# Two units of a fused attention and feed-forward kernel go up together before they go down, with fewer memsets in the front

## The chip, the cores and the metric

One core of a Trainium2 chip runs the whole program. The metric is device time in microseconds (us). Before the change the median of three runs was 217.9 us (217.55 to 217.96). The profile counts from the first to the last instruction, which is a little shorter: 216.0 us in the profiled run.

Each run also lists the mean clock that was granted to TensorE. A run counts as slow if it is over 1.5% above the fastest run of its kernel; only fast runs are compared. A ratio here is the mean time of one kernel's fast runs over the mean of the other's fast runs in the same rounds on the same chip, so it is not quite the ratio of the medians that are quoted. The interval behind a ratio is its 95% interval.

## The reference, cut to what matters

```python
# attention: B=4, H=8, S=768, D=64; chunks of 32 queries, 16 keys to the left,
# 8 to the right, and 8 memory keys for each head
for c in range(S // 32):
    k_full = concat([mem_k, k[max(0, 32*c - 16) : min(S, 32*c + 40)]])   # v likewise
    out[c] = softmax(q_c @ k_full.T / sqrt(D)) @ v_full
x = out.transpose(0, 2, 1, 3).reshape(B, S, 512)
# feed-forward
xn = (x - mean) / sqrt(var + 1e-6) * g_ln
y = x + relu(xn @ w_ch1) @ w_ch2          # 512 -> 2048 -> 512
```

## The kernel before

The work is cut into 24 tiles of 128 tokens, and three tiles make a unit. A tile passes through **scores** (K times Q on TensorE, exponent on ScalarE), **values** (TensorE), **norm** (VectorE) and **turn_x** (transposes on TensorE, then a copy out of PSUM on ScalarE). A unit then goes **up** (16 products with W1 for each tile, four from each of W1's four quarters) and **down** (4 parts a tile with W2). In the traces of this case TensorE runs these pieces in program order (in the kernel before, a wait of 0.55 us at 29.31 holds all that follows), so the order in which the program lists these pieces is the schedule.

```python
att = [ps.tile([128, 2, 512], FP32, name=f"att{i}") for i in range(2)]  # PSUM: scores, values, transposes
mm = [ps.tile([128, 512], FP32, name=f"mm{i}") for i in range(4)]       # PSUM: up, down

def norm(t, xi):                     # VectorE; p is the att buffer of values(t)
    nc.vector.reciprocal(out=r, in_=free(p, 64, [[128, H]]))
    nc.vector.scalar_tensor_tensor(out=x, in0=p, ..., accum_out=total[i])
    nc.vector.tensor_scalar(out=nmean[i], ...)
    nc.vector.scalar_tensor_tensor(out=xn[i], in0=x, scalar=nmean[i], in1=g_row, ...)

def turn_x(u, i, t, kind="att"):
    pv = ...                         # next att buffer, or a bank of mm
    for dt in range(4):
        nc.tensor.matmul(out=pv[...], lhsT=xn[t % 3][...], rhs=identity, is_transpose=True, ...)
    nc.scalar.copy(out=xT[u % 2][:, :, 128 * i : 128 * i + 128], in_=...)

def up(u, n, hc, t0=0, on_act=False):     # tiles t0 to n-1 of unit u, block hc of 16
    p = slot("mm")[:, 0 : hi - lo]
    for dt in range(4):
        nc.tensor.matmul(out=p, lhsT=..., rhs=xT[u % 2][:, dt, lo:hi], ...)
    # Relu out of PSUM to rT[hc]: odd hc on ScalarE, even hc on VectorE
```

The front (cut to order) clears buffers on VectorE, keeps TensorE busy with filler matmuls (`stay_busy`) while K and Q arrive, attends the first three tiles and takes them up as W1 arrives:

```python
    stay_busy(10)
    clear_v(0, nc.vector, lambda: clear_q(0, 0))
    clear_q(0, 1)
    clear_k(0)
    mem_keys()
    mem_cols(0)
    stay_busy(4)
    # ... loads: W1 quarters 0 to 3, rest of K and Q, W2 with V groups between ...
    turn_x(0, 2, 2)
    for hc in range(4, 8):
        up(0, 2, hc)
    for hc in range(8):
        up(0, 3, hc, 2)
```

Then comes a loop over the units. It takes 16 steps of up and 12 of down, and hangs the attention of the next unit's tiles on the steps of down:

```python
attend(((16, 19, 19, 22), (17, 19, 20, 23), (21, 23, 23, 26)), "att")   # unit 1's plan for unit 2:
                                   # for each tile the steps of scores, values, norm, turn_x
```

The softmax here doesn't subtract the row's maximum and nothing guards it: scores larger than these inputs give would overflow.

Of the kernel before, what the change touches and what calls it, by code (L numbers as in the profile page):

```python
# [15 lines left out]
def kernel(  # L16
# [43 lines left out]
    qraw = [sb.tile([128, 4096], FP16, name=f"qraw{i}") for i in range(2)]  # L60
    QT = kraw[1]
    k16 = [t[0:96, 0:4096].rearrange("p (h r d) -> p h r d", h=H, r=8) for t in kraw]
    q16 = [t[0:96, 0:4096].rearrange("p (h r d) -> p h r d", h=H, r=8) for t in qraw]
# [7 lines left out]
    rT = [sb.tile([128, 384], FP16, name=f"rT{hc}") for hc in range(16)]  # L71
    osb = [sb.tile([128, 512], FP32, name=f"osb{i}") for i in range(3)]
    total = [sb.tile([128, 1], FP32, name=f"total{i}") for i in range(3)]
    nmean = [sb.tile([128, 1], FP32, name=f"nmean{i}") for i in range(3)]
# [29 lines left out]
    def load_kq(b, which, lo=0, hi=96, h0=0, h1=H):  # L104

        dst, src = ((k16, k), (q16, q))[which]
        nc.gpsimd.dma_start(
            out=dst[b % 2][lo:hi, h0:h1, :, :],
            in_=dram(src, (b * H + h0) * HS + 512 * lo,
                     [[512, hi - lo], [HS, h1 - h0], [1, 512]]),  # L110
        )
# [97 lines left out]
    def kq_block(b, j, g0, g1, kind, last=nc.scalar.copy):  # L209
# [7 lines left out]
        for i in range(2):  # L217
            turn_kq(as16(pk[:, i, :]), k16[b % 2], j + i, 96)
        for i in range(2):
            turn_kq(as16(pq[i]), q16[b % 2], j + i, 96)  # L220
# [19 lines left out]
    def load_tokens(b, which, t):  # L240
        dst, src = ((kraw[0], k), (qraw[0], q))[which]
# [11 lines left out]
    def cross_q(half, t0, t1):  # L253
        nc.sync.dma_start_transpose(
            out=free(QT, (24 * half + 4 * t0) * 64, [[64, 4 * (t1 - t0)], [1, 64]]),
            in_=qraw[0][64 * half : 64 * half + 64, 512 * t0 : 512 * t1],
# [59 lines left out]
    def norm(t, xi):  # L316
# [10 lines left out]
            out=nmean[i], in0=total[i], scalar1=-1.0 / 512, scalar2=None, op0=ALU.mult,  # L327
        )
        nc.vector.scalar_tensor_tensor(  # L329
            out=xn[i], in0=x, scalar=nmean[i], in1=g_row, op0=ALU.add, op1=ALU.mult,  # L330
        )

    def root(t, xi):
        i = t % 3
        nc.scalar.activation(  # L335
            out=junk, in_=xs[xi], func=ACTF.Square, bias=nmean[i], accum_out=squares[i],
# [33 lines left out]
    def up(u, n, hc, t0=0, on_act=False):  # L370
# [10 lines left out]
        o = rT[hc][:, lo:hi]  # L381
# [7 lines left out]
    def down(t, i, part):  # L389
# [3 lines left out]
        for hc in range(4 * part, 4 * part + 4):  # L393
            nc.tensor.matmul(  # L394
                out=p, lhsT=rT[hc][:, 128 * i : 128 * i + 128],
# [10 lines left out]
    def down_last(t, i):  # L406

        o = osb[t % 3]
        for lo, hi in ((0, 256), (256, 384), (384, 512)):
            p = slot("mm")[:, 0 : hi - lo]  # L410
            for hc in range(16):
                nc.tensor.matmul(  # L412
                    out=p, lhsT=rT[hc][:, 128 * i : 128 * i + 128],
# [20 lines left out]
    def clear_q(i, par):  # L434

        nc.vector.memset(QZ[i][64 - 64 * par : 128 - 64 * par, :, :, par, :], 0.0)  # L436

    def clear_v(i, eng, between=lambda: None):
# [3 lines left out]
        eng.memset(V[i][:, :, :, 64:HD], 1.0)  # L442
# [20 lines left out]
    nc.vector.memset(memv16[:, :, :, 64:HD], 1.0)  # L463
# [12 lines left out]
    clear_v(0, nc.vector, lambda: clear_q(0, 0))  # L476
    clear_q(0, 1)
    clear_k(0)
    mem_keys()
    mem_cols(0)  # L480
    stay_busy(4)
# [14 lines left out]
    for c in range(4):  # L496
        load_w1(c)
    for which in range(2):
        load_kq(0, which, CUT[which], 96)
    load_w2(0)  # L500
    load_w2(1)
    for g in range(6, 10):
        load_v_group(0, g)
    load_w2(2)
    for g in range(10, NG):
        load_v_group(0, g)
    load_w2(3)
# [11 lines left out]
    for j in range(2):  # L519
        turn_kq(first_k[j], k16[0], j, CUT[0])  # L520
    for j in range(2):
        turn_kq(first_q[j], q16[0], j, CUT[1])
# [5 lines left out]
    for j in range(2, 4):  # L528
        turn_kq(first_k[j], k16[0], j, CUT[0])
# [3 lines left out]
    for j in range(2, 4):  # L533
        turn_kq(first_q[j], q16[0], j, CUT[1])
# [5 lines left out]
    nc.vector.tensor_copy(out=g_row, in_=banks[2])  # L540
    scores(0, 0)
# [21 lines left out]
    turn_x(0, 2, 2)  # L563
    for hc in range(4, 8):
        up(0, 2, hc)
    for hc in range(8):
        up(0, 3, hc, 2)
# [3 lines left out]
    for u, tiles in enumerate(units):  # L571
        n = len(tiles)
        following = units[u + 1] if u + 1 < len(units) else []
        plan = {}

# [3 lines left out]
        def attend(steps, kind="dma"):  # L579

            for i, (s0, s1, s2, s3) in enumerate(steps):
# [5 lines left out]
                at(min(s3 + 3, 27), root, t % 6, t % 9)  # L587
# [11 lines left out]
        if u == 0:  # L599
            at(7, clear_q, 1, 0)  # L600
            at(9, clear_q, 1, 1)
            at(10, clear_k, 1)
            at(23, clear_v, 1, nc.gpsimd)
            for j in (0, 2):
                at(15, kq_block, 0, j, 6, NG, "mm", nc.vector.tensor_copy if j else nc.scalar.copy)
                at(15, keep_rest)
            for t in range(3):
                at(19 + t, root, t, t)
# [96 lines left out]
```

## Time and profile before

| | before |
|---|---|
| median of three runs | 217.9 us |
| span of the profiled run | 216.0 us |
| TensorE (PE) busy | 97% of the span |
| VectorE (DVE), ScalarE (ACT), GpSimd (POOL) busy | 55%, 46%, 48% |
| TensorE's share of the chain that ended last | 94% |

The page's picture in 40 slices of 5.4 us each shows the same in time. Each digit is PE's busy share in tenths, and 9 means 90% or more:

```profile
span 216.0 us, 5059 instructions
...
PE   7999989999999999999999999999999999999993
```

Only the first slice, the sixth (from 27.0 to 32.4 us, with the wait of 0.55 us) and the last show any slack. PE is the bound, and a change can win only what PE waits or spends on fillers.

### The profile page before, as it was taken

The page shows a single profiled execution, that of the slowest core. Times are in us where ns is not written, and L with a number is a line of the kernel's source. Part 1 is how long each engine was busy: PE and PEld are TensorE (multiplying, and loading weights), DVE is VectorE, ACT ScalarE, POOL GpSimd, SP SyncE. Part 2 cuts the span into 40 slices and gives each one's busy share as a digit, 9 for nine tenths or more (in the row PEclk, how much of TensorE's full clock was granted, in tenths as well). Part 3 has the DMA queues.
Part 4 walks back from the last instruction along what each step waited for, and adds up shares of the span by engine and source line. Part 5 has one row for each costly group of instructions (what it writes and reads, how often), then busy time and mean ns, then how long its engine had stood idle before and what let it go on. Part 6 is the DMA issues. An engine that isn't in the chain of part 4 may idle for free.

```text
span 216.0 us, 5059 instructions
## 1 busy us (share of the span) xinstructions
PE 210.2 (97%) x2011; PEld 129.8 (60%) x2011; DVE 118.6 (55%) x274; ACT 99.7 (46%) x206; POOL 104.4 (48%) x185
## 2 busy tenths in 40 slices
PE   7999989999999999999999999999999999999993
PEld 2557866557765577546754676456754675466562
DVE  6967675685737548524375349224484447634222
ACT  4478437855893677302653167103761275314100
POOL 7993245699996318974004998507145000400000
PEclk9999999999999999999999999999999999999998
DMA  5999999999999989996312999997674101330012
GB/s 78 182 150 207 209 208 181 200 206 226 148 140 172 102 135 146 151 146 171 48 27 80 142 186 148 138 156 103 176 150 132 49 3 24 91 108 0 0 49 100
DMA packets 87714, 27.37 MB, mean 127 GB/s; under 512 B 78297, under 2 KB 84185, under 8 KB 87642
## 3 DMA queue, kind: packets, MB, share of 16 engines
q0 software_dynamic: 62128, 14.38, 78.2%
q1 hardware_dynamic: 25562, 12.66, 28.2%
q8 instruction: 16, 0.26, 0.5%
q14 instruction: 8, 0.07, 0.1%
HBM read 28.84 MB, written 6.29 MB: 163 GB/s over the span
## 4 chain that ended last, share of the span: by engine, by line
PE 94%; DVE 3%; ACT 1%; issue 1%; ACTq 0%
PE mm L377 37%; PE mm L394 37%; PE att L289 5%; PE att L309 3%; PE mm L366 3%; PE att L179 2%; PE mm L412 2%; PE mm L179 1%; DVE QZ L436 1%; ACT AT L296 1%; PE att L352 1%; PE att L366 1%; DVE rT L385 1%; PE mm L539 0%; DVE xn L329 0%
## 5 line engine op out<-in xcount | busy, mean ns | idle before, releaser
L377 PE MATMUL mm<-xT,w1c 128*128 128x384 f16 (+2 forms) x560 | 89.0, 313 | 0.6 <-DVE rT L385 0.6
L394 PE MATMUL mm<-w2c,rT 128*128 128x512 f16 x368 | 84.4, 379 | 0.0
L377 PEld LDWEIGHTS <-w1c 128*128 128x128 f16 x560 | 58.8, 114 | 23.6 <-issue 1.0
L383 ACT ACTIVATE rT<-mm 128x384 f16<-128x384 f32 (+2 forms) x74 | 33.1, 453 | 72.4 <-PE mm L377 50.2
L394 PEld LDWEIGHTS <-rT 128*128 128x128 f16 x368 | 34.7, 98 | 37.5
L385 DVE TENSOR_SCALAR rT<-mm 128x384 f16<-128x384 f32 (+2 forms) x66 | 34.9, 533 | 33.6 <-PE mm L377 33.5
L401 DVE SCALAR_TENSOR_TENSOR osb<-mm,rstd,xs 128x512 f32<-128x512 f32 x23 | 17.3, 750 | 41.8 <-PE mm L394 24.9
L296 ACT ACTIVATE AT<-att,band 104x512 f16<-104x512 f32 x48 | 30.2, 683 | 9.6 <-PE att L289 8.2
L338 POOL TENSOR_SCALAR veps<-squares 128x1 f32<-128x1 f32 x24 | 4.8, 200 | 42.7 <-ACT junk L335 41.3
L117 POOL DMA_DIRECT2D V<-in_v_dram x24 | 18.4, 772 | 11.0 <-DMA w1c<-in_moe_w_ch_dram 7.8
L335 ACT ACTIVATE junk<-xs,nmean 128x512 f16<-128x512 f32 x24 | 17.3, 721 | 7.1 <-DVE nmean L326 6.7
L329 DVE SCALAR_TENSOR_TENSOR xn<-xs,nmean,g_row 128x512 f16<-128x512 f32 x24 | 18.8, 782 | 0.9
L320 DVE SCALAR_TENSOR_TENSOR xs<-att,rec 128x512 f32<-128x512 f32 x24 | 16.6, 691 | 0.8
L289 PEld LDWEIGHTS <-KT 128*128 128x128 f16 x192 | 12.6, 98 | 4.6 <-issue 1.0
L277 POOL COPY QZ<-kraw 64x768 f16<-64x768 f16 x16 | 13.2, 826 | 3.9 <-DMA kraw<-qraw 3.4
L342 POOL TENSOR_TENSOR rstd<-veps,mhalf 128x1 f32<-128x1 f32 x24 | 13.7, 571 | 2.0
L289 PE MATMUL att<-QZ,KT 128*128 128x128 f16 x192 | 14.6, 219 | 0.0
L269 POOL COPY KT<-KT 128x128 f16<-128x128 f16 (+4 forms) x16 | 4.2, 292 | 18.2 <-DMA KT<-kraw 18.1
L123 POOL DMA_DIRECT2D V<-in_v_dram x16 | 12.0, 791 | 0.9 <-PE mm L377 0.7
L309 PEld LDWEIGHTS <-AT 104*64 104x64 f16 x384 | 7.5, 111 | 6.5 <-ACT AT L296 2.1
L242 POOL DMA_DIRECT2D qraw<-in_q_dram x12 | 11.3, 938 | 0.0
L242 POOL DMA_DIRECT2D kraw<-in_k_dram x12 | 11.2, 934 | 0.0
(76 smaller groups left out, 136.6 us busy)
## 6 DMA issues: line engine op xcount, KB each, us to landing
out_dram<-osb SPq DMA_DIRECT2D x23, 256.0 KB, 2.3
V<-in_v_dram POOLq DMA_DIRECT2D x36, 96.0 KB, 6.9
w1c<-in_moe_w_ch_dram POOLq DMA_DIRECT2D x4, 512.0 KB, 9.6
w2c<-in_moe_w_ch_dram POOLq DMA_DIRECT2D x4, 512.0 KB, 13.5
kraw<-in_k_dram POOLq DMA_DIRECT2D x12, 128.0 KB, 5.3
qraw<-in_q_dram POOLq DMA_DIRECT2D x12, 128.0 KB, 5.4
qraw<-in_q_dram POOLq DMA_DIRECT2D x3, 384.0 KB, 11.6
kraw<-in_k_dram POOLq DMA_DIRECT2D x3, 256.0 KB, 5.7
```

What stands on the lines that cost most here:

```text
L117: nc.gpsimd.dma_start(out=V[b % 2][r : r + hi - lo, g, :, 0:64], in_=dram(v, b * H * HS + lo * D, [[64, hi - lo], [HS, H], [1, 64]]),)
L242: nc.gpsimd.dma_start(out=free(dst, 512 * t, [[64, H], [1, 64]]), in_=dram(src, b * H * HS + 128 * t * D, [[D, 128], [HS, H], [1, 64]]),)
L289: nc.tensor.matmul(out=p[:, gg, 128 * j : 128 * j + 128], lhsT=KT[b % 2][:, (4 * g + j) * KW : (4 * g + j) * KW + 128], rhs=QZ[b % 2][:, g ...
L296: nc.scalar.activation(out=free(a, 32 * c, [[512, 2], [64, 8], [1, 32]], KR), in_=free(p, 32 * c, [[512, 2], [64, 8], [1, 32]], KR), func= ...
L320: nc.vector.scalar_tensor_tensor(out=x.rearrange("p (h d) -> p h d", h=H), in0=free(p, 0, [[128, H], [1, 64]]), scalar=1.0, in1=free(r, 0, ...
L329: nc.vector.scalar_tensor_tensor(out=xn[i], in0=x, scalar=nmean[i], in1=g_row, op0=ALU.add, op1=ALU.mult,)
L335: nc.scalar.activation(out=junk, in_=xs[xi], func=ACTF.Square, bias=nmean[i], accum_out=squares[i],)
L377: nc.tensor.matmul(out=p, lhsT=free(w, i, [[4, 128]]), rhs=xT[u % 2][:, dt, lo:hi], start=(dt == 0), stop=(dt == 3),)
L383: nc.scalar.activation(out=o, in_=p, func=ACTF.Relu)
L385: nc.vector.tensor_scalar(out=o, in0=p, scalar1=0.0, scalar2=None, op0=ALU.max)
L394: nc.tensor.matmul(out=p, lhsT=rT[hc][:, 128 * i : 128 * i + 128], rhs=w2c[hc // 4][:, hc % 4, :], start=(hc == 0), stop=(hc == 15),)
L401: nc.vector.scalar_tensor_tensor(out=o, in0=p, scalar=rstd[t % 9], in1=xs[t % 9], op0=ALU.mult, op1=ALU.add,)
```

## The change

The intent is to have PE follow W1's quarters as they land: units 0 and 1 both go up first, with the attention of unit 1 between the quarters, and then both go down. It also takes memset time off VectorE in the front, so that the first tile is ready sooner. It needs a second set of `rT`, and lays ten of its sixteen tiles over `kraw[1]`, so that K and Q of odd batches share one raw buffer with the even ones.

```diff
-        eng.memset(V[i][:, :, :, 64:HD], 1.0)
+        eng.memset(V[i].bitcast(FP32)[:, :, :, 32 : HD // 2], TWO_ONES)   # two fp16 ones as one fp32
...
-    clear_v(0, nc.vector, lambda: clear_q(0, 0))
-    clear_q(0, 1)
-    clear_k(0)
+    nc.vector.memset(memv16[:, :, :, 64:HD], 1.0)
+    clear_v(0, nc.vector, lambda: (clear_q(0, 0, 0, 6), clear_q(0, 1, 0, 6), clear_k(0)))
     mem_keys()
     mem_cols(0)
-    stay_busy(4)
...
-    for c in range(4):
-        load_w1(c)
+    load_w1(0)
     for which in range(2):
         load_kq(0, which, CUT[which], 96)
...                        # then W1 1, V 6-7, W1 2, V 8-11, W1 3, W2 0-3
     nc.vector.tensor_copy(out=g_row, in_=banks[2])
+    for par in range(2):
+        clear_q(0, par, 6, NG)
...
     turn_x(0, 2, 2)
+    for hc in range(4):
+        up(0, 3, hc, 2)
+    for j in (0, 2):
+        kq_block(0, j, 6, NG, "mm", vec if j else act)
+        keep_rest()
     for hc in range(4, 8):
-        up(0, 2, hc)
-    for hc in range(8):
-        up(0, 3, hc, 2)
+        up(0, 3, hc)
+    scores(0, 3)
+    up(0, 3, 8)
+    scores(0, 4)
+    up(0, 3, 9)
+    values(0, 3)
+    norm(3, 3)
+    up(0, 3, 10)
+    values(0, 4)
+    norm(4, 4)
+    up(0, 3, 11)
+    scores(0, 5)
+    turn_x(1, 0, 3)
+    for hc in range(4):
+        up(1, 1, hc)
+    values(0, 5)
+    norm(5, 5)
+    turn_x(1, 1, 4)
+    for hc in range(4):
+        up(1, 2, hc, 1)
+    for hc in range(12, 16):
+        up(0, 3, hc)
+    turn_x(1, 2, 5)
+    for hc in range(4):
+        up(1, 3, hc, 2)
...                        # the loop starts at unit 1, step 4, and takes 24 downs
-            attend(((16, 19, 19, 22), (17, 19, 20, 23), (21, 23, 23, 26)), "att")
+                at(24 + 2 * j, kq_block, 1, j, 0, NG, "att")
+                at(26 + 2 * j, keep_rest)
+            attend(((30, 32, 32, 35), (30, 33, 33, 36), (34, 36, 36, 39)), "att")
```

More of the change, by code (lines that the diff above doesn't have):

```diff
@@ L59 @@
     kraw = [sb.tile([128, 4096], FP16, name=f"kraw{i}") for i in range(2)]
-    qraw = [sb.tile([128, 4096], FP16, name=f"qraw{i}") for i in range(2)]
+    qraw = sb.tile([128, 4096], FP16, name="qraw")
     QT = kraw[1]
-    k16 = [t[0:96, 0:4096].rearrange("p (h r d) -> p h r d", h=H, r=8) for t in kraw]
-    q16 = [t[0:96, 0:4096].rearrange("p (h r d) -> p h r d", h=H, r=8) for t in qraw]
+    k16, q16 = [t[0:96, :].rearrange("p (h r d) -> p h r d", h=H, r=8) for t in (kraw[0], qraw)]
     V = [sb.tile([128, NG, H, HD], FP16, name=f"V{i}") for i in range(2)]
@@ L70 @@
     xT = [sb.tile([128, 4, 384], FP16, name=f"xT{i}") for i in range(2)]
-    rT = [sb.tile([128, 384], FP16, name=f"rT{hc}") for hc in range(16)]
+    rT = [[sb.tile([128, 384], FP16, name=f"rT{hc}") for hc in range(16)],
+          [kraw[1][:, 384 * hc : 384 * hc + 384] for hc in range(10)]
+          + [sb.tile([128, 384], FP16, name=f"rT1_{hc}") for hc in range(10, 16)]]
     osb = [sb.tile([128, 512], FP32, name=f"osb{i}") for i in range(3)]
     total = [sb.tile([128, 1], FP32, name=f"total{i}") for i in range(3)]
-    nmean = [sb.tile([128, 1], FP32, name=f"nmean{i}") for i in range(3)]
+    nmean = [sb.tile([128, 1], FP32, name=f"nmean{i}") for i in range(9)]
     squares = [sb.tile([128, 1], FP32, name=f"squares{i}") for i in range(3)]
@@ L107, in load_kq @@
         nc.gpsimd.dma_start(
-            out=dst[b % 2][lo:hi, h0:h1, :, :],
+            out=dst[lo:hi, h0:h1, :, :],
             in_=dram(src, (b * H + h0) * HS + 512 * lo,
@@ L217, in kq_block @@
         for i in range(2):
-            turn_kq(as16(pk[:, i, :]), k16[b % 2], j + i, 96)
+            turn_kq(as16(pk[:, i, :]), k16, j + i, 96)
         for i in range(2):
-            turn_kq(as16(pq[i]), q16[b % 2], j + i, 96)
+            turn_kq(as16(pq[i]), q16, j + i, 96)
         def keep(i):
@@ L240, in load_tokens @@
     def load_tokens(b, which, t):
-        dst, src = ((kraw[0], k), (qraw[0], q))[which]
+        dst, src = ((kraw[0], k), (qraw, q))[which]
         nc.gpsimd.dma_start(
@@ L255, in cross_q @@
             out=free(QT, (24 * half + 4 * t0) * 64, [[64, 4 * (t1 - t0)], [1, 64]]),
-            in_=qraw[0][64 * half : 64 * half + 64, 512 * t0 : 512 * t1],
+            in_=qraw[64 * half : 64 * half + 64, 512 * t0 : 512 * t1],
         )
@@ L326, in norm @@
         nc.vector.tensor_scalar(
-            out=nmean[i], in0=total[i], scalar1=-1.0 / 512, scalar2=None, op0=ALU.mult,
+            out=nmean[xi], in0=total[i], scalar1=-1.0 / 512, scalar2=None, op0=ALU.mult,
         )
         nc.vector.scalar_tensor_tensor(
-            out=xn[i], in0=x, scalar=nmean[i], in1=g_row, op0=ALU.add, op1=ALU.mult,
+            out=xn[i], in0=x, scalar=nmean[xi], in1=g_row, op0=ALU.add, op1=ALU.mult,
         )
@@ L335, in root @@
         nc.scalar.activation(
-            out=junk, in_=xs[xi], func=ACTF.Square, bias=nmean[i], accum_out=squares[i],
+            out=junk, in_=xs[xi], func=ACTF.Square, bias=nmean[xi], accum_out=squares[i],
         )
@@ L380, in up @@
             )
-        o = rT[hc][:, lo:hi]
+        o = rT[u == 1][hc][:, lo:hi]
         if hc % 2 or on_act:
@@ L394, in down @@
             nc.tensor.matmul(
-                out=p, lhsT=rT[hc][:, 128 * i : 128 * i + 128],
+                out=p, lhsT=rT[t // 3 == 1][hc][:, 128 * i : 128 * i + 128],
                 rhs=w2c[hc // 4][:, hc % 4, :],
@@ L412, in down_last @@
                 nc.tensor.matmul(
-                    out=p, lhsT=rT[hc][:, 128 * i : 128 * i + 128],
+                    out=p, lhsT=rT[0][hc][:, 128 * i : 128 * i + 128],
                     rhs=w2c[hc // 4][:, hc % 4, lo:hi],
@@ L432, in clear_k, with clear_q @@
         nc.vector.memset(KT[i][:, end : end + 32], 0.0)
-    def clear_q(i, par):
-        nc.vector.memset(QZ[i][64 - 64 * par : 128 - 64 * par, :, :, par, :], 0.0)
+    def clear_q(i, par, g0=0, g1=NG):
+        nc.vector.memset(QZ[i][64 - 64 * par : 128 - 64 * par, g0:g1, :, par, :], 0.0)
+    TWO_ONES = (2.0 ** -7) * (1 + 15 * 2.0 ** -13)
     def clear_v(i, eng, between=lambda: None):
@@ L462 @@
     nc.vector.memset(mhalf, -0.5)
-    nc.vector.memset(memv16[:, :, :, 64:HD], 1.0)
     nc.sync.dma_start(out=memk32, in_=dram(mem_k, 0, [[64, 128], [128 * 64, 2], [1, 64]]))
@@ L495 @@
     nc.gpsimd.tensor_tensor(out=band[:, 1:2], in0=band[:, 1:2], in1=zero3[:, 2:3], op=ALU.add)
-    for c in range(4):
-        load_w1(c)
+    load_w1(0)
     for which in range(2):
         load_kq(0, which, CUT[which], 96)
-    load_w2(0)
-    load_w2(1)
-    for g in range(6, 10):
+    load_w1(1)
+    for g in range(6, 8):
         load_v_group(0, g)
-    load_w2(2)
-    for g in range(10, NG):
+    load_w1(2)
+    for g in range(8, NG):
         load_v_group(0, g)
-    load_w2(3)
+    load_w1(3)
+    for c in range(4):
+        load_w2(c)
     nc.gpsimd.dma_start(
@@ L519 @@
     for j in range(2):
-        turn_kq(first_k[j], k16[0], j, CUT[0])
+        turn_kq(first_k[j], k16, j, CUT[0])
     for j in range(2):
-        turn_kq(first_q[j], q16[0], j, CUT[1])
+        turn_kq(first_q[j], q16, j, CUT[1])
     for j in range(2):
@@ L528 @@
     for j in range(2, 4):
-        turn_kq(first_k[j], k16[0], j, CUT[0])
+        turn_kq(first_k[j], k16, j, CUT[0])
     for j in range(2, 4):
@@ L533 @@
     for j in range(2, 4):
-        turn_kq(first_q[j], q16[0], j, CUT[1])
+        turn_kq(first_q[j], q16, j, CUT[1])
     for g0, g1 in ((0, 2), (2, 6)):
@@ L563 @@
     turn_x(0, 2, 2)
-    for hc in range(4, 8):
-        up(0, 2, hc)
-    for hc in range(8):
-        up(0, 3, hc, 2)
+    for hc in range(4):
[3 more added lines that the diff above has]
+        keep_rest()
+    for hc in range(4, 8):
+        up(0, 3, hc)
[23 more added lines that the diff above has]
+        up(1, 3, hc, 2)
     units = [[t, t + 1, t + 2] for t in range(0, 6 * B, 3)]
-    for u, tiles in enumerate(units):
+    for u, tiles in list(enumerate(units))[1:]:
         n = len(tiles)
+        down_tiles = units[0] + units[1] if u == 1 else tiles
         following = units[u + 1] if u + 1 < len(units) else []
         plan = {}
+        last = 15 + 4 * len(down_tiles)
         def at(step, fn, *args):
@@ L586, in attend @@
                 at(s3, turn_x, u + 1, i, t % 6, kind)
-                at(min(s3 + 3, 27), root, t % 6, t % 9)
+                at(min(s3 + 3, last), root, t % 6, t % 9)
         def cross(steps, b, t0, t1, t2):
@@ L597, in spread @@
                 at(step + half, spread_q, b, half, t0, t1)
-        if u == 0:
-            at(7, clear_q, 1, 0)
-            at(9, clear_q, 1, 1)
+        if u == 1:
+            at(6, clear_q, 1, 0)
+            at(8, clear_q, 1, 1)
             at(10, clear_k, 1)
-            at(23, clear_v, 1, nc.gpsimd)
-            for j in (0, 2):
-                at(15, kq_block, 0, j, 6, NG, "mm", nc.vector.tensor_copy if j else nc.scalar.copy)
-                at(15, keep_rest)
-            for t in range(3):
-                at(19 + t, root, t, t)
+            at(5, clear_v, 1, nc.gpsimd)
+            for t in range(6):
+                at(13 + 2 * t, root, t, t)
             for h in (0, 4):
                 for which in range(2):
-                    at(15, load_kq, 1, which, 0, 96, h, h + 4)
-            for g in range(6):
-                at(23, load_v_group, 1, g)
-            attend(((17, 19, 19, 22), (18, 21, 21, 24), (20, 23, 23, 26)), "att")
-            at(26, mem_cols, 1)
-            at(26, v_mem, 1)
-        elif u == 1:
+                    at(4, load_kq, 1, which, 0, 96, h, h + 4)
+            at(16, mem_cols, 1)
+            at(16, v_mem, 1)
+            for g in range(NG):
+                at(24, load_v_group, 1, g)
             for j in (0, 2):
-                at(5 + 3 * j, kq_block, 1, j, 0, NG, "att")
-                at(7 + 3 * j, keep_rest)
-            for g in range(6, NG):
-                at(0, load_v_group, 1, g)
+                at(24 + 2 * j, kq_block, 1, j, 0, NG, "att")
+                at(26 + 2 * j, keep_rest)
             for t in range(6):
                 for which in range(2):
-                    at(14, load_tokens, 2, which, t)
-            attend(((16, 19, 19, 22), (17, 19, 20, 23), (21, 23, 23, 26)), "att")
+                    at(30, load_tokens, 2, which, t)
+            attend(((30, 32, 32, 35), (30, 33, 33, 36), (34, 36, 36, 39)), "att")
         elif following:
@@ L660 @@
                 spread(3, 3, 3, 6)
-        for step in range(16 + 4 * n):
+        for step in range(4 if u == 1 else 0, last + 1):
             if step < 16:
-                if u or step > 7:
-                    up(u, n, step)
+                up(u, n, step)
             else:
                 i, part = divmod(step - 16, 4)
-                if u == 0:
-                    i, part = (step - 16) % 3, (step - 16) // 3
                 if following or i < n - 1:
-                    down(tiles[i], i, part)
+                    down(down_tiles[i], i % n, part)
                 elif part == 0:
```

## The prediction

> **What bounds the kernel now.** I read the engines' busy line and the chain that ended last, then the chain in order of time, then the timeline where the change works. First the page:
>
> ```profile
> PE 210.2 (97%) x2011; PEld 129.8 (60%) x2011; DVE 118.6 (55%) x274; ACT 99.7 (46%) x206; POOL 104.4 (48%) x185
> ...
> PE 94%; DVE 3%; ACT 1%; issue 1%; ACTq 0%
> ```
>
> TensorE (PE) carries 94% of the chain, so only time in which PE waits or does filler can be won. The chain in order of time (start, length, what, count) shows where that is:
>
> ```profile
> 18.34 0.79 PE mm L377 x12
> ...
> 21.08 0.22 PE att L352 x4
> 21.31 3.32 PE mm L377 x44
> ...
> 29.31 1.46 PE mm L377 x8
> 30.77 0.80 PE att L179 x32
> ...
> 73.72 0.22 PE att L352 x4
> 73.95 0.86 PE mm L394 x4
> 74.81 1.95 PE mm L377 x12
> ```
>
> L377 is the product with W1 ("up"), L394 that with W2 ("down"), L352 the transpose of a normalised tile, L179 the turning of K and Q. At 74.81 unit 2 begins; from there on the programs are alike, so the prediction is when unit 2 begins after the change. Note what follows each L352: another matmul that doesn't need the turned tile (44 ups of older tiles at 21.31; one down at 73.95). Those hide the copy of the tile on ScalarE. The timeline gives what a transpose costs without that, and the other costs used below:
>
> ```profile
> 18.10 0.80 POOL L117 DMA_DIRECT2D V<-in_v_dram  x1 [1.75 <-DMA w1c<-in_moe_w_ch_dram]
> ...
> 18.97 0.39 PE L352 MATMUL att<-identity,xn 128*128 128x128 f16 x4
> 19.39 0.58 ACT L357 COPY xT<-att 128x512 f16<-128x512 f16 x1
> 20.03 1.05 PE L377 MATMUL mm<-xT,w1c 128*128 128x128 f16 x16
> ...
> 27.51 1.34 DVE L436 MEMSET QZ<- 64x1536 uint32 x1 [0.26 <-issue]
> 28.91 0.78 POOL L117 DMA_DIRECT2D V<-in_v_dram  x1 [0.90 <-DMA qraw<-in_q_dram]
> 29.31 1.46 PE L377 MATMUL mm<-xT,w1c 128*128 128x384 f16 x8 [0.55 <-DVE rT L385]
> ...
> 38.55 0.21 DVE L319 RECIPROCAL rec<-att 128x8 f32<-128x8 f32 x1 [3.23 <-ACT AT L296]
> 39.79 0.75 DVE L329 SCALAR_TENSOR_TENSOR xn<-xs,nmean,g_row 128x512 f16<-128x512 f32 x1
> ...
> 52.95 1.60 ACT L204 COPY QZ<-att 64x768 f16<-64x768 f16 x2 [0.99 <-PE att L179]
> 54.96 1.58 ACT L204 COPY QZ<-att 64x768 f16<-64x768 f16 x2
> ```
>
> Transpose to first use of it: 20.03 - 18.97 = 1.06 us, of which PE works 0.22 to 0.39, so some 0.7 is idle unless filled. A norm on VectorE: 38.55 to 40.54, 1.9 to 2.0 us, and it has read its PSUM buffer after 0.95. PE's only wait for another engine after 20.1 is 0.55 us, behind two memsets. No wait of PE is ended by a weight quarter; W1's land at 17.8 (first issue 10.83 plus the shortest landing, 7.0), about 20.5, 23.1 and 26.2, as the waits of the V loads end.
>
> **What the skill says.** "TensorE: Matmul & The Clock Gate", section "Step-by-step: what each phase is for": only weight loads are pulled ahead, matmuls keep program order. So one matmul that waits holds all later ones; the 0.55 us above, with nothing slipped in, agrees. Same page, "Why this matters for your kernels": gaps above about 3 us cost the clock; the waits that I find are under 1.5 us, and the granted clock before was 1.00 in every stretch up to 200 us. "VectorE: DVE Perf Modes", "Zero memsets can be issued as uint32 (trn2)": a memset's time goes by elements, not bytes. The trace agrees (1338 ns for 1536 elements, f16 or uint32), so writing the ones as fp32 pairs halves that memset.
>
> **The change part by part.**
>
> Front, VectorE. The ones memset falls from 1536 elements to 768 (1.34 to about 0.67 us), two QZ memsets are halved (2.68 to 1.34), their other halves come after g_row; the rest only changes places. VectorE reaches its first K copy about 1.5 us earlier (8.9 to 7.4), four filler matmuls (1.4 us) go. But the four first loads of K and Q land at 5.5, 7.0, 8.5 and 9.5 us in the trace, which the turns must await, and the first up needs W1's first quarter, which lands at 17.8 as before; it starts at 18.27 now. Also the two delayed half memsets (1.6 us with gaps) stand right before the first norm, which has only 1.33 us of idle before it. I give the front 0.1 to 0.4 us, and take 0.1.
>
> Loads. New order after quarter 0: rest of K and Q, quarter 1, V 6 and 7, quarter 2, V 8 to 11, quarter 3, W2. With 2.5 us a quarter, 2.5 for the rest of K and Q (26.4 to 28.9) and 0.63 a V group (W2's second to third quarter, 5.0 us, less 2.5, over four): 20.3, 22.8, 24.1, 26.6, 29.1, 31.6, W2 complete at 41.6. PE wants them at 22.8, 25.6, 30.4, 28.7, 36.3, 39.0, 52: all in time, so the loads bind neither way.
>
> PE's work. The same ups, downs, scores and turns, only in another order. With an up of three tiles 0.65 us, of one tile 0.225, a pair of turning blocks 2.85, scores 0.45, values 0.37, I walk PE's order from the built program:
>
> 1. Transpose of tile 2 at 21.0; next come ups of that tile alone: they start at 21.9, 0.7 idle. Ups end 22.8, turning of K and Q 25.6, ups 4 to 7 (banks freed by the copies just in time) 28.25.
> 2. Scores 3, up 8, scores 4, up 9, values 3: its norm runs 31.0 to 32.9 on VectorE. Behind it in VectorE's order stand one up eviction (0.5), then norm 4: 33.4, and its PSUM buffer is read only at 34.35. The transpose of tile 3 takes that very buffer. PE is through with scores 5 at 33.1: 1.25 idle. Then the copy: 0.7 to 0.85 idle, ups from 35.4 to 36.3.
> 3. Values 5, transpose of tile 4 at 36.7, copy exposed: ups from 37.65 (0.7 idle) to 38.55. Their eviction stands behind norm 5 (36.8 to 38.7), so up 12 waits for its bank until 39.05: 0.5 idle. Ups 12 to 15 end 41.7.
> 4. Transpose of tile 5, copy behind an eviction: 42.65, 0.7 idle. One-tile ups to 43.55, twelve full ups 7.8, the two 1.34 us memsets between their evictions again cost 0.55: 51.9.
> 5. Downs. Unit 1's took 74.81 - 61.14 = 13.67 with attention; twelve more at 0.864 are 10.4, two turning blocks of 1.48 are 2.96: 27.0. But scores of unit 2 now come two downs (1.73) after the second turning block, and need all four QZ copies, 1.60 + 1.58 on ScalarE: 1.4 idle. And unit 2's last transpose stands at the last step with no down behind it: 0.7 idle. Unit 2 starts at 51.9 + 27.0 + 2.1 = 81.0.
>
> **The same as a sum:** exposed transposes 5 x 0.7 = 3.5, the PSUM buffer 1.25, the bank 0.5, the QZ copies 1.4, together 6.65; less the front's 0.1 to 0.4; the 0.55 cancels. 81.0 - 74.8 = 6.2 us more, 217.9 + 6.2 = 224.1. I put it at 224.0.
>
> **Rivals.** (a) The change does what it means to: PE, fed quarter by quarter, starts steady work sooner. Then the most to be won is the waits and fillers behind 18.3 us: 0.55, filler 0.43, the front 0.4, some 1.4 us: 216.5, within 2%. Against it: PE waits for no quarter before the change. (b) The loads bind: a quarter that slips (before, the fourth took 3.3 instead of 2.5) behind V groups would stop up 8, whose slack is 2.1 us, or a late K and Q the turning, slack 2.5. It would add 1 or 2 us on top: 226. For it: the load queues are 90% busy there. (c) The clock: with four fillers fewer, PE could wake later (in the timeline the fillers fall from 0.43 to about 0.26 us each at 6.7). One late window costs perhaps 1 to 1.5 us of front; W1's landing hides part. (d) Batch 2's tokens, now loaded behind twelve V groups, arrive late for unit 2. V loads can go out from about 58, twelve at 0.78, then twelve token loads at 0.88: 78, landed by 81. Unit 2 uses them from 81 on: nothing lost by this sum; a slip costs perhaps 1 us.
>
> **Range and chances.** Each of the eight idle pieces is an order of instructions on one engine, read off the built program, so I trust their sign; sizes may be off by a third: 6.65 +- 2.2. Rivals (b) and (c) lengthen the tail upward, (a) downward. Range 220.5 to 227.0. The 2% line is 222.3, which is 4.4 us more: two thirds of my sum. Slower by over 2%: 0.70; within: 0.26; faster: 0.04, as the 4.4 us that it needs are not there to win.
>
> **What would show it.** In the profile after: unit 2's first full up near 81 instead of 74.8; PE's busy time almost as before but idle gaps of about 0.7 before L378 after each L353 (the shifted lines), one of 1.2 before the transpose of tile 3 released by VectorE, one near 1.4 in the downs released by ScalarE's QZ copies; no PE wait ended by a weight load. I am wrong if PE runs dense from 22 to 52 us, if W1 or W2 ends its waits, if the first up starts well before 17.8, or if the clock falls in a gap.

## The result, and the profile after

The changed kernel is correct and slower. Its median is 226.66 us over four runs (225.31 to 227.81), against 217.73 us for the kernel before in the same rounds. The ratio is 1.041, interval 1.035 to 1.0471.

The page of the kernel after:

```profile
span 224.8 us, 5086 instructions
PE 210.6 (94%) x2023; PEld 130.0 (58%) x2023; DVE 119.0 (53%) x278; ACT 100.4 (45%) x208; POOL 104.2 (46%) x185
...
PE   7887995899997989999999999999999999999993
...
PE 72%; DMA 7%; DVE 6%; SPq 5%; POOL 4%; issue 3%; ACT 2%; POOLq 0%; DVEq 0%
```

PE is busy for 210.6 us instead of 210.2. The span grew by 8.8 us, so PE waits 8.4 us more in all. But the total hides a shift: in front of the first up, where the four fillers went, PE is busy 1.3 us less, and from the first up to unit 2's first up it is busy 1.5 us more. The view `--windows` shows that stretch (from and to, its length, then PE's busy time, and the other engines), before and then after:

```profile
18.27:74.81 56.54, 55.97 (x713) 37.47 (x708) 36.87 (x89) 36.59 (x77) 37.80 (x58) 1.00 1.60 183
```

```profile
18.85:82.69 63.84, 57.48 (x723) 37.87 (x723) 36.83 (x90) 36.97 (x79) 36.26 (x58) 1.00 1.37 160
```

So the stretch grew by 7.30 us: 5.79 us of it are waits and 1.51 us are PE's own time. The ups account for 1.0 us of the latter: their busy time there went from 22.4 to 23.4 us, as the change cuts them smaller (96 matmuls of one tile, where before there were 64 of one tile and 16 of two); the other 0.5 us was not traced, and as the ends of matmuls are modelled, the split is good to some tenths. With the first up 0.58 us later and 0.92 us more behind unit 2's first up, this makes the 8.8 us.

The slices show where the waits are: nearly all the low digits stand in the first fifteen slices, up to unit 2. PE's share of the chain fell from 94% to 72%. Part of that is only the way in which the chain is followed back, since it now passes through other engines at each new wait.

PE's timeline names every wait. The columns are start, length, engine, line, operation, out<-in, shapes and count; the bracket is the idle time before the group and what ended it. L378 is up, L353 the transposes of turn_x, L290 scores, L310 values.

```profile
18.85 0.86 PE L378 MATMUL mm<-xT,w1c 128*128 128x128 f16 x12 [0.92 <-DMA w1c<-in_moe_w_ch_dram]
...
22.55 1.05 PE L378 MATMUL mm<-xT,w1c 128*128 128x128 f16 x16 [0.67 <-ACT xT L358]
...
35.19 0.38 PE L353 MATMUL att<-identity,xn 128*128 128x128 f16 x4 [1.03 <-DVE xs L321]
36.25 1.05 PE L378 MATMUL mm<-xT,w1c 128*128 128x128 f16 x16 [0.67 <-ACT xT L358]
...
38.68 1.05 PE L378 MATMUL mm<-xT,w1c 128*128 128x128 f16 x16 [0.67 <-ACT xT L358]
39.95 2.76 PE L378 MATMUL mm<-xT,w1c 128*128 128x384 f16 x16 [0.23 <-DVE kraw L386]
...
43.77 7.56 PE L378 MATMUL mm<-xT,w1c 128*128 128x128 f16 x56 [0.83 <-ACT xT L358]
51.74 1.46 PE L378 MATMUL mm<-xT,w1c 128*128 128x384 f16 x8 [0.41 <-DVE rT L386]
...
70.80 0.89 PE L290 MATMUL att<-QZ,KT 128*128 128x128 f16 x13 [0.94 <-ACT QZ L205]
...
82.69 2.11 PE L378 MATMUL mm<-xT,w1c 128*128 128x384 f16 x12 [0.67 <-ACT xT L358]
94.95 1.46 PE L378 MATMUL mm<-xT,w1c 128*128 128x384 f16 x8 [0.54 <-DVE rT L386]
```

Five of the groups wait for `xT`, the copy on ScalarE of a tile that PE has just transposed: 4 x 0.67 + 0.83 = 3.51 us. The line at 35.19 waits for VectorE to have read a PSUM buffer. The one at 70.80 waits for the copies of Q, after another 0.21 us for K at 69.54 that is not shown. The line at 82.69 is unit 2's first up, which began at 74.81 before (so in the chain view, which cuts overlaps; the timeline draws that group from 74.65, over the end of the one before it). The waits at 18.85 (W1's first quarter) and 94.95 (in unit 2) were not in the prediction's walk.

The same walk as a table, with the predicted times from the prediction's steps and the measured ones from this timeline and its neighbouring lines:

| point in PE's order | predicted | measured | late by |
|---|---|---|---|
| first up (18.27 less 0.1) | 18.17 | 18.85 | 0.68 |
| first up after the transpose of tile 2 | 21.9 | 22.55 | 0.65 |
| turning of K and Q | 22.8 | 23.54 | 0.74 |
| scores 3 | 28.25 | 29.06 | 0.81 |
| transpose of tile 3 | 34.35 | 35.19 | 0.84 |
| transpose of tile 4 | 36.7 | 37.60 | 0.90 |
| up 12 | 39.05 | 39.95 | 0.90 |
| first up after the transpose of tile 5 | 42.65 | 43.77 | 1.12 |
| first down | 51.9 | 53.04 | 1.14 |
| unit 2's first up | 81.0 | 82.69 | 1.69 |

Of the 1.69 us that the walk was late, 0.68 were there at its first point.

Two waits on VectorE's own timeline after. The first shows why the PSUM buffer came free late:

```profile
33.07 0.75 DVE L330 SCALAR_TENSOR_TENSOR xn<-xs,nmean,g_row 128x512 f16<-128x512 f32 x1
33.74 0.55 DVE L386 TENSOR_SCALAR rT<-mm 128x384 f16<-128x384 f32 x1
34.20 0.20 DVE L320 RECIPROCAL rec<-att 128x8 f32<-128x8 f32 x1
34.44 0.69 DVE L321 SCALAR_TENSOR_TENSOR xs<-att,rec 128x512 f32<-128x512 f32 x1
```

The norm of tile 3 ends with the line at 33.07, an eviction of an up follows, and only then the norm of tile 4 reads its buffer, to 35.13. The transposes that take this buffer start at 35.19. This is the order that the prediction's step 2 gives.

The second is the wait in unit 2 at 94.95. The same copy of memory keys on VectorE, in the kernel before and then after:

```profile
85.56 0.33 DVE L169 COPY KT<-memKT 128x384 f16<-128x384 f16 x1
```

```profile
93.55 0.88 DVE L170 COPY KT<-memKT 128x384 f16<-128x384 f16 x1
```

It took 0.55 us longer, and the up eviction behind it came that much later, which is the size of PE's gap.

### The profile page after: what moved, and what is told of

It reads as the page before. It is cut to its first block, busy times and chain, and to the rows that moved or that the text cites. A ratio compares the mean times of both kernels' runs of the same rounds, so it can differ in the third digit from the quotient of the medians.

```text
span 224.8 us, 5086 instructions
## 1 busy us (share of the span) xinstructions
PE 210.6 (94%) x2023; PEld 130.0 (58%) x2023; DVE 119.0 (53%) x278; ACT 100.4 (45%) x208; POOL 104.2 (46%) x185
## 4 chain that ended last, share of the span: by engine, by line
PE 72%; DMA 7%; DVE 6%; SPq 5%; POOL 4%; issue 3%; ACT 2%; POOLq 0%; DVEq 0%
PE mm L395 31%; PE mm L378 30%; DMA w1c<-in_moe_w_ch_dram 4%; PE att L290 3%; SPq L249 3%; DMA V<-V 3%; PE att L310 3%; PE att L180 2%; POOL V L118 2%; PE mm L413 2%; DVE xs L321 1%; ACT QZ L205 1%; DVE QZ L437 1%; SPq L255 1%; ACT xT L358 1%
## 5 line engine op out<-in xcount | busy, mean ns | idle before, releaser
L378 PE MATMUL mm<-xT,w1c 128*128 128x384 f16 (+1 forms) x576 | 90.0, 309 | 5.6 <-ACT xT L358 3.5
L395 PE MATMUL mm<-w2c,rT 128*128 128x512 f16 x338 | 76.1, 379 | 0.0
L378 PEld LDWEIGHTS <-w1c 128*128 128x128 f16 x576 | 59.0, 114 | 28.7 <-issue 5.8
L384 ACT ACTIVATE rT<-mm 128x384 f16<-128x384 f32 (+1 forms) x67 | 30.4, 458 | 74.6 <-PE mm L378 52.5
L395 PEld LDWEIGHTS <-rT 128*128 128x128 f16 x338 | 32.5, 98 | 37.1
L386 DVE TENSOR_SCALAR rT<-mm 128x384 f16<-128x384 f32 (+1 forms) x59 | 31.9, 545 | 35.9 <-PE mm L378 35.9
L290 PEld LDWEIGHTS <-KT 128*128 128x128 f16 x192 | 12.5, 98 | 5.4 <-issue 2.6
L290 PE MATMUL att<-QZ,KT 128*128 128x128 f16 x192 | 14.5, 219 | 1.1 <-ACT QZ L205 0.9
L343 POOL TENSOR_TENSOR rstd<-veps,mhalf 128x1 f32<-128x1 f32 x24 | 13.2, 550 | 2.0
L270 POOL COPY KT<-KT 128x128 f16<-128x128 f16 (+4 forms) x16 | 4.8, 326 | 18.6 <-DMA KT<-kraw 18.6
L205 ACT COPY QZ<-att 64x768 f16<-64x768 f16 (+1 forms) x12 | 8.2, 686 | 9.8 <-PE att L180 9.7
L243 POOL DMA_DIRECT2D kraw<-in_k_dram x12 | 11.6, 970 | 0.0
```

The source lines that it names most:

```text
L243: nc.gpsimd.dma_start(out=free(dst, 512 * t, [[64, H], [1, 64]]), in_=dram(src, b * H * HS + 128 * t * D, [[D, 128], [HS, H], [1, 64]]),)
L290: nc.tensor.matmul(out=p[:, gg, 128 * j : 128 * j + 128], lhsT=KT[b % 2][:, (4 * g + j) * KW : (4 * g + j) * KW + 128], rhs=QZ[b % 2][:, g ...
L378: nc.tensor.matmul(out=p, lhsT=free(w, i, [[4, 128]]), rhs=xT[u % 2][:, dt, lo:hi], start=(dt == 0), stop=(dt == 3),)
L384: nc.scalar.activation(out=o, in_=p, func=ACTF.Relu)
L386: nc.vector.tensor_scalar(out=o, in0=p, scalar1=0.0, scalar2=None, op0=ALU.max)
L395: nc.tensor.matmul(out=p, lhsT=rT[t // 3 == 1][hc][:, 128 * i : 128 * i + 128], rhs=w2c[hc // 4][:, hc % 4, :], start=(hc == 0), stop=(hc ...
```

## The experiments

Eight kernels ran, in two sets (no run is labelled e8); all gave a correct result. The theory was that the change loses by uncovered waits on PE, each of which can be filled. The rivals were the clock, the order of the loads, and the front.

### e1_front: the front's memsets alone

Only the front's part is put into the kernel before.

```diff
+        eng.memset(V[i].bitcast(FP32)[:, :, :, 32 : HD // 2], TWO_ONES)   # in place of fp16 ones
-    clear_v(0, nc.vector, lambda: clear_q(0, 0))
-    clear_q(0, 1)
-    clear_k(0)
+    nc.vector.memset(memv16[:, :, :, 64:HD], 1.0)
+    clear_v(0, nc.vector, lambda: (clear_q(0, 0, 0, 6), clear_q(0, 1, 0, 6), clear_k(0)))
-    stay_busy(4)
     nc.vector.tensor_copy(out=g_row, in_=banks[2])
+    for par in range(2):
+        clear_q(0, par, 6, NG)
```

Expected:

> The kernel before with the front part of the change alone (smaller and later memsets on VectorE, four filler matmuls gone). My theory: this part is good for 0.1 to 0.4 us and no more, because the first up waits for W1's first quarter, which lands at 17.8 us either way; so the time falls from 217.7 to about 217.4 and the first up starts at 17.9 to 18.2 instead of 18.27. Rival (the front itself costs, by a clock that wakes late or by memsets in front of the first norm): the first up starts later than 18.3 and the time rises by 0.5 us or more.

Measured: median 218.34 us over six runs (216.85 to 221.91), and 217.84 for the kernel before. The ratio of fast runs is 0.9995, interval 0.9951 to 1.0039. In its profile the first up starts at 17.85 instead of 18.27 and the span is 215.1 instead of 216.0, so the front gives about 0.4 us at the first up there; the rest of the 0.9 us was not traced. Two of the six runs were slow: 221.91 us at a clock of 0.977, and 221.88 us at a clock of 1.0, which nothing here explains. What follows: the front's part doesn't make the change slow, and what it wins is too small to show in the times.

### e2_exposed: one transpose uncovered in the kernel before

```diff
-            attend(((16, 19, 19, 22), (17, 19, 20, 23), (21, 23, 23, 26)), "att")
+            attend(((16, 19, 19, 22), (17, 19, 20, 23), (21, 23, 23, 27)), "att")
```

The transpose of unit 2's last tile moves behind the last down, so nothing is left to cover its copy.

> The kernel before with one thing moved: unit 1's last tile is transposed after the last down instead of before it, so that nothing stands between the transpose and the first up of unit 2. My theory, that an uncovered transpose costs TensorE some 0.7 us: a gap of 0.67 us before the first up of unit 2 released by the copy on ScalarE, and 217.7 + 0.7 = 218.4. Rival (the gap is only shifted and caught up later, or covered by a weight load): within 0.2 us of 217.7.

Measured: 218.41 us (217.98 to 219.28), ratio 1.0034, interval 0.9999 to 1.0069; 0.0034 of 217.84 is 0.74 us, but the interval just reaches 1, so the time alone doesn't show it. PE's timeline has the one new gap, at unit 2's start:

```profile
75.60 1.62 PE L377 MATMUL mm<-xT,w1c 128*128 128x384 f16 x9 [0.67 <-ACT xT L357]
```

Unit 2 begins at 75.60 instead of 74.81; 0.12 of these 0.79 us were there at the first up already (18.39 instead of 18.27). One uncovered transpose costs about 0.7 us where it stands. This is the unit in which the prediction counted, and the gap is measured here with nothing else changed.

### e3_fill: the changed kernel with its front's waits filled

PE's order in the front is changed so that other ready work follows each transpose. The change's order of loads and of units is kept. Not shown in the cut: two more ups of unit 1 go into the front, so the loop starts two steps later, and the loads of batch 1's K and Q and the clearing of its V go two steps later with it.

```diff
     turn_x(0, 2, 2)
+    kq_block(0, 0, 6, NG, "mm", act)
+    keep_rest()
     for hc in range(4):
         up(0, 3, hc, 2)
-    for j in (0, 2):
-        kq_block(0, j, 6, NG, "mm", vec if j else act)
-        keep_rest()
+    kq_block(0, 2, 6, NG, "mm", vec)
+    keep_rest()
...
+    up(0, 3, 12)
+    up(0, 3, 13)
     turn_x(1, 0, 3)
-    for hc in range(4):
-        up(1, 1, hc)
+    up(0, 3, 14)
     values(0, 5)
     norm(5, 5)
+    for hc in range(4):
+        up(1, 1, hc, 0, True)
     turn_x(1, 1, 4)
+    up(0, 3, 15)
...                        # likewise behind turn_x(1, 2, 5)
```

> The changed kernel with TensorE's order in the front altered, all else kept: the first turning block of K and Q behind the transpose of tile 2, ups 12 to 15 of unit 0 spread behind the transposes of tiles 3 and 4, two ups of two tiles behind that of tile 5, and one-tile evictions of unit 1 on ScalarE. My theory, that the loss is waits which other work could cover: the gaps of 0.67, 1.03, 0.67, 0.67, 0.23 and 0.83 us in the profile after, 4.1 us together, go, and the time falls from 226.7 to about 222.6. Rival (the loss is W1's late landing, or is in the amount of work): gaps move to waits for weights, and the time stays above 225.5.

Measured: median 224.01 us, in two groups. Two fast runs took 221.58 and 222.9 us. Two slow runs took 225.12 and 225.57 us at a clock of 0.977. The ratio of fast runs is 1.0204, interval 1.0143 to 1.0266, so some 4.4 us less than the change (222.24, the mean of the two, against its 226.6). The profile fell into a slow run; its granted clock by slices, and a stretch of 6 us with the busy time of each engine, the clock, the DMA share and GB/s:

```profile
PEclk9757999999999999999999999999999999999999
```

```profile
9.00:15.00 6.00, 6.00 (x74) 3.00 (x73) 2.50 (x7) 2.37 (x7) 5.46 (x16) 0.50 2.78 145
```

The clock was half from 8.9 to 19.1 us. The gaps behind the transposes in the front are gone, and from the first up to unit 2's first up this profile needs 82.10 - 21.92 = 60.2 us, against 82.69 - 18.85 = 63.8 in the changed kernel. The clock was back to full by then, so these 3.6 us come from the filling. The times of this run are less firm than the sign.

### e4_fill_downs: the waits in the downs filled too

On top of e3_fill, unit 1's turning of K and Q goes four steps earlier and its attention one step earlier. That leaves downs between the turning and the scores, and one down behind the last transpose.

```diff
-                at(24 + 2 * j, kq_block, 1, j, 0, NG, "att")
-                at(26 + 2 * j, keep_rest)
+                at(20 + 2 * j, kq_block, 1, j, 0, NG, "att")
+                at(22 + 2 * j, keep_rest)
...
-            attend(((30, 32, 32, 35), (30, 33, 33, 36), (34, 36, 36, 39)), "att")
+            attend(((29, 31, 31, 34), (29, 32, 32, 35), (33, 35, 35, 38)), "att")
```

> As the run before it, and in the downs of units 0 and 1 the turning blocks of batch 1 come four steps earlier and the attention of unit 2 one step earlier. My theory: the waits of 0.21 and 0.94 us for K and Q copies and of 0.67 us for the last transpose go too, 1.8 us: about 220.8. Rival (those waits cover a slow load or copy that then shows elsewhere): less than 0.7 us below the run before it.

Measured: 219.77, 219.77 and 219.54 us, and one slow run of 223.7 at a clock of 0.969. The ratio is 1.0087, interval 1.0043 to 1.0132. What waits PE has left from the first up on:

```profile
18.50 0.86 PE L378 MATMUL mm<-xT,w1c 128*128 128x128 f16 x12 [0.49 <-DMA w1c<-in_moe_w_ch_dram]
24.71 0.38 PE L378 MATMUL mm<-xT,w1c 128*128 128x128 f16 x4 [0.60 <-ACT QZ L205]
47.80 1.46 PE L378 MATMUL mm<-xT,w1c 128*128 128x384 f16 x8 [0.41 <-DVE rT L386]
69.05 0.41 PE L310 MATMUL att<-V,AT 104*64 104x65 f16 x15 [0.41 <-DMA V<-in_v_dram]
```

The waits for `xT`, for the PSUM buffer and for the copies of Q before the scores are gone. Unit 2's first up comes at 77.21 instead of 82.69, and the gap in unit 2 is gone as well. With the order of loads and of units of the change kept, and the ups cut no larger, some 7 of its 8.9 us have come back. So the waits are the cause of most of the loss. Even filled, this order stays 1.9 us (0.0087 x 217.84) behind the kernel before. Waits explain only about half of that. From the first up to unit 2's first up PE is busy for 57.10 of 58.71 us here, against 55.97 of 56.54 in the kernel before: it waits 1.0 us more and works 1.1 us more. The second part is the rival "amount of work" of e3_fill, and filling can't bring it back; the ups take 24.2 us in that stretch, against 22.4.

### e5_own_bank: another buffer for one transpose

The 1.03 us at 35.19 were put down to the PSUM buffer. Here the transpose takes a bank of `mm` instead.

```diff
-    turn_x(1, 0, 3)
+    turn_x(1, 0, 3, "mm")
```

> The changed kernel, where the transpose of tile 3 writes into one of the four PSUM banks of the ups instead of the attention buffer that the norm of tile 4 still reads. My theory, that this one buffer held TensorE 1.03 us: that gap goes or shrinks to what the norm of tile 3 leaves (0.2 us), the ups that follow begin about 1 us sooner, the time falls from 226.7 to about 225.8. Rival (the gap is owed to VectorE's chain of two norms whatever the buffer): the same gap before the next instruction that needs a norm, no gain at unit 2's first up.

Measured: 225.56 us (225.36 to 228.13, the last at a clock of 0.977), ratio 1.0371, interval 1.0327 to 1.0416, against 218.01 us before. The transpose now starts at 33.65 at once, and the wait moves behind it. PE's line, and ScalarE's timeline of the same stretch:

```profile
35.69 1.05 PE L378 MATMUL mm<-xT,w1c 128*128 128x128 f16 x16 [1.65 <-ACT xT L358]
```

```profile
33.90 1.26 ACT L297 ACTIVATE AT<-att,band 104x512 f16<-104x512 f32 x2
35.05 0.58 ACT L358 COPY xT<-mm 128x512 f16<-128x512 f16 x1
```

The copy of the tile stands behind the exponent of the scores that PE had just made, so PE waits 1.65 us instead of 1.03 + 0.67 = 1.70. From the first up to unit 2's it takes 82.07 - 18.51 = 63.56 us, against 63.84: 0.28 won, not 1.0. The buffer was truly awaited, but it hid another wait of nearly the same length. As a cause of lost time it was named too narrowly.

### e6_loads: quarter 1 of W1 ahead of the rest of K and Q

```diff
     load_w1(0)
+    load_w1(1)
     for which in range(2):
         load_kq(0, which, CUT[which], 96)
-    load_w1(1)
```

> The changed kernel with W1's second quarter loaded before the rest of K and Q, as in the kernel before. In the profile after, the first quarter landed at 18.8 us instead of 17.8 and TensorE waited 0.92 us for it. If the order of loads does that: it lands at 17.8 again, the first up starts 0.6 to 0.9 us sooner, the rest of K and Q lands at 22.8 to 23 and is just in time for its turn at 22.9, and the time falls from 226.7 to about 225.9. If the late landing is chance: it lands at 18.5 or later here too, and there is no gain.

Measured: median 229.27 us (226.24 to 232.76), ratio of fast runs 1.0428, interval 1.0376 to 1.0479. Three of the four runs had a clock between 0.97 and 0.985, and the profiled one was among them, with half clock from 11.6 to 18.4 and from 38.9 to 45.7 us. Quarter 0 landed at 18.43 us there, no better than in two other kernels with the changed order of loads (18.46 each). Its one run at full clock took 226.24 us, which lies among the changed kernel's times. The run doesn't show that the order of loads matters, and with that clock it can't show that it doesn't.

### e7_moved: the best of both

The kernel before takes the front's memsets, keeps two of the four fillers, now placed between the turning of K and of Q, and moves the memsets that made its 0.55 us wait to steps at which VectorE has time.

```diff
+    stay_busy(2, spare)                     # between turn_kq of K and of Q; stay_busy(4) goes
...
-            at(7, clear_q, 1, 0)
-            at(9, clear_q, 1, 1)
-            at(10, clear_k, 1)
+            at(16, clear_q, 1, 0)
+            at(16, clear_q, 1, 1)
+            at(25, clear_k, 1)
```

> The kernel before with the front's smaller memsets, two of the four fillers kept (between the turns of K and Q, where TensorE waits for Q anyway), and the two memsets of batch 1's Q moved from between the up evictions of unit 0 into its downs, where VectorE sits idle for 3.2 us. My theory: the first up starts 0.3 us sooner, the gap of 0.55 us at 29 us goes, so 217.8 falls to about 217.0, and no run has a lowered clock. Rival (what is won in front is caught up in the downs, where W2's quarters land as late as before): within 0.2 us of 217.8.

Measured: 217.11 us (216.46 to 219.17), against 218.01: ratio 0.997, interval 0.9934 to 1.0007, no slow run. The 0.55 us wait is gone from PE's timeline, and between the first up and the end no gap is left. What remains in front of it:

```profile
18.33 0.86 PE L377 MATMUL mm<-xT,w1c 128*128 128x128 f16 x12 [0.35 <-DMA w1c<-in_moe_w_ch_dram]
```

This is the fastest kernel by its median, by 0.9 us, but the interval just reaches 1. It shows how little there was to win: with PE dense from the first up on, the time is still about 217.

### e9_fillers: the changed kernel with the four fillers back

```diff
     mem_keys()
     mem_cols(0)
+    stay_busy(4)
     v_mem(0)
```

> The changed kernel with the four filler matmuls of the front put back. The run with filled waits had two of four runs with a granted clock of 0.977, and in its profile the clock was at half from 9 to 19 us; the front alone on the kernel before had two slow runs of six. If the missing fillers are the cause: no run here below a clock of 0.99, and the time as the changed kernel's, 226 to 227, since its four runs had none of the low clocks. If they are not: low clocks turn up here as well. The rival of the whole study, that the clock makes the change slow, would need a fall by 3 us or more here.

Measured: 225.94 us (225.37 to 226.62) at clocks of 0.998 to 1.0, ratio 1.0358, interval 1.0327 to 1.0389. PE's timeline has the same gaps as the changed kernel's. Up to unit 2 all agree to 0.01 us but the first, the wait for W1's quarter, which is 0.81 here. Unit 2 begins at 82.62. With a full clock the loss stays, so the clock is not its cause.

## Why the prediction was right

The prediction said 224.0 us, 220.5 to 227.0, slower with a chance of 0.70. The result was 226.66: slower, and inside the range near its upper end. Point by point:

- **Nothing to win at the front end of W1.** Right. PE was not waiting for quarters before the change, and e7_moved, with PE dense, ends near 217. Rival (a) falls.
- **Front, 0.1 to 0.4 us.** Right in e1_front (0.42 at the first up), but the changed kernel kept none of it. VectorE began its first norm at 14.60 instead of 14.94 us, and then PE waited 0.92 us for W1's first quarter.
- **"W1's first quarter, which lands at 17.8 as before".** This step failed, and by the prediction's own words ("I am wrong ... if W1 or W2 ends its waits") the wait of 0.92 us counts against it. The quarter landed at 18.80, and 0.68 of the walk's 1.69 us came from there. In the kernels that load all of W1 first it landed at 17.82, 17.75, 17.77 and 18.28; in those with the changed order at 18.80, 18.56, 18.46, 18.46, 18.73 and 18.43. That is an association with the order, 0.67 us on the mean, but e6_loads didn't separate the parts of the order, so what delays the tail of the quarter stays open. Rival (b) named a late quarter, but another one: quarters 1 to 3 and W2 ended no wait of PE.
- **Five uncovered transposes, 3.5 us.** Measured 3.51, and e2_exposed confirmed the unit price.
- **The PSUM buffer, 1.25 us.** Measured 1.03, released as step 2 said. The sum is right, but e5_own_bank shows that freeing the buffer alone wins 0.28.
- **The bank, 0.5 us.** Measured 0.23. **The copies of Q, 1.4 us.** Measured 0.94 + 0.21 (K's copy) = 1.15. **The memset wait, 0.55 us, cancels.** Measured 0.41 after.
- **"The same ups, downs, scores and turns, only in another order".** This is the term that was mis-sized most. All waits of the walk together were 7.20 us (6.65 and the 0.55) and measured 6.33, so they were over-estimated by 0.9 us, and still the walk was late. It left 62.83 - 7.20 = 55.6 us for PE's own pieces between the first up and unit 2; they took 63.84 - 6.33 = 57.5, 1.9 us more. Four ups of one tile took 0.98 to 1.05 us where the walk used 0.9, and four transposes with nothing behind them take 0.39 until the copy may start, where the walk mostly used 0.22. These two are seen in the lines; how the last 0.55 us in the downs divides was not separated. The sum has no term for PE's own time at all: less the front's 0.1 it gives 6.55, and the 6.2 that was used comes from the walk.
- **"From there on the programs are alike".** Nearly: unit 2 to the end took 142.1 instead of 141.2 us. 0.54 of this is the wait at 94.95 behind the slow copy on VectorE and 0.28 a wait for V at 164.38. The copy took 0.88, 0.88 and 0.95 us in the changed kernel, e5_own_bank and e9_fillers, and 0.25 to 0.45 in e3_fill and e4_fill_downs. In units 2 and 4 every such copy of over 0.3 us ran beside a load issue or a copy of GpSimd, but so did some of 0.25 us. Why is open.
- **Rival (c), the clock.** Not in the changed kernel's four runs (0.992 to 0.998) nor in e9_fillers, but it is real in its relatives, as the last section tells. **Rival (d), late tokens.** No wait of PE before unit 2 was ended by them.

The sum of the errors is 1.69 up to unit 2 and 0.9 behind it, 2.6 us, which is the difference between 224.0 and 226.66. Up to unit 2 it is made of 0.68 for the late quarter and 1.9 for PE's own pieces, less 0.9 for the waits. The mechanism, uncovered waits, was right, and it carries 5.8 of the 8.8 us; PE's own time and the quarter were missed. That the number still fell inside the range is partly luck: with the waits sized as measured, the same prediction and range would have lain 0.9 us lower, and 226.66 outside.

## What to carry to other kernels

When one engine is busy for 97% of the time in program order, judge a reordering by what follows each of its hand-offs: every transpose needs work behind it that doesn't depend on it, for as long as the other engine takes to copy (here 0.7 us). Count the pieces too: the same ups in smaller ones cost PE 1.0 us here. Feeding the engine as weights land wins nothing where no wait was ended by weights. When you remove a wait, look for the next one behind it before you count the gain, as e5_own_bank shows.

## What the Trainium skill lacked or had wrong

- **A clock that falls without a long gap.** "TensorE: Matmul & The Clock Gate", sections "What's actually happening" and "Why this matters for your kernels", ties a halved clock to idle times of about 3 us and more, and its section "A second HAM failure mode: psum-queue depth-cycling" says without a length that short idle times between groups can do it too. In the profile of e3_fill the clock was half from 8.9 to 19.1 us, and the longest gap of PE after its first matmul was 0.69 us until then. In e6_loads it was half again from 38.9 to 45.7 us, right behind waits of 1.03 and 0.67 us; the changed kernel's profile has the same waits at a full clock. PE's busy time between 5 and 8.5 us was 2.88 us there and 2.61 in e6_loads, whose clock fell too, against 3.50 in the kernel before; but it was 2.78 in the changed kernel's profile, where the clock held (these times count the transposes of K and Q too). Kernels without the four fillers had a granted clock below 0.99 in 8 of 26 runs; the kernel before and the kernels that keep fillers had none. The pair that differs in the fillers alone, the changed kernel and e9_fillers, had 0 of 4 each, so this is an association and not proof.
- **Memsets of a constant other than zero.** "VectorE: DVE Perf Modes", "Zero memsets can be issued as uint32 (trn2)", speaks of zeros. Ones written as fp32 pairs gained as much: the row of that memset went from 1.34 to 0.70 us. The page's one cycle an element, 1.04 ns at its clock of 0.96 GHz, is not shown wrong: the row of 1536 elements reads 0.87 ns each, but from the start of such a memset to the start of the next it is 1.72 us (3.08 to 4.80), and for 768 elements 0.89 to 0.92, so 768 elements more cost some 0.8 us, about 1.07 ns each.
- **The landing of the first of several queued loads.** No page gives it: the same first quarter of W1, issued at 10.8 us in each, landed between 17.75 and 18.80 us, on the mean 0.67 us later in the kernels with the changed order of loads behind it.
